# A Linformer attention and MLP-mixer kernel: the first pair's k and v as float32 over two hardware queues, and a new order for the opening

## The chip, the cores and the metric

The kernel runs on one core of a Trainium2 chip. The metric is the device time of one execution in microseconds (us), as the median of several runs. The engines have short names in the profile: PE is TensorE, PEld its weight loads, DVE is VectorE, ACT is ScalarE, POOL is GpSimd and SP is SyncE. A q behind a name (SPq, POOLq) means the engine's instruction sequencer.

## The reference, cut to what matters

```
k_proj = einsum('ks,bhsd->bhkd', E, k)          # q, k, v: 8 x 8 x 1024 x 64
v_proj = einsum('ks,bhsd->bhkd', F, v)          # E, F: 64 x 1024
attn   = softmax(q @ k_proj^T / 8)              # rows of 64 keys
x      = (attn @ v_proj), heads side by side    # 8 x 1024 x 512
h      = relu(x^T @ w_tok1) @ w_tok2            # mixing over the 1024 tokens, 256 wide
u      = x + h^T
out    = u + relu(u @ w_ch1) @ w_ch2            # mixing over the 512 channels, 1536 wide
```

All inputs and the output are float32.

## The kernel before, in words

The batch has eight elements, and each passes through the same stages: the projections of k and v with E and F (`kv_proj`, products in line 521), the transposes of the projected k (`k_transpose`, 574) and of q (`q_transpose_pe`, 618, for the first elements), the scores (637) with their exponential on ACT (652), the product with the projected v (`attend`, 672), whose extra column gives the sum of each row, a reciprocal of that sum (686) and a scaling multiply (692) on DVE that write x. Then come the two products over the tokens, and for each half of 512 tokens (a row block, j from 0 to 15) an up block (1180) and a down block (1289) over the channels, which use seven products of half-size quarters in place of eight. The down block's results are added to u on DVE and stored from the tiles o0, o1 and o2 (1326).

Heads go in pairs, g from 0 to 3 (heads 2g and 2g+1). For batch element 0 the front is done pair by pair, with a token product by parts (`token1_part` 1060, `token2_part` 1092, `u_transpose_pe` 1121), so that the first up block can begin early. The pair g=1, heads 2 and 3, is worked on first.

**What sets the order.** Each piece of work is a job that is handed to a planner (`Planner`, line 116) with its engine and what it reads and writes. The planner schedules nothing any more: the string ORDER lists all jobs in the order in which they are issued, two characters for each job (its number in base 64), SPOTS gives the PSUM bank of each bank user, and FILLS lists the places in that order at which an idle product of zeros (`blank`, line 435) is issued ahead of a PE job. `pin` ties each instruction to the one before it on its engine, so every engine runs its jobs strictly in this order.

**Loads.** k, v, q and the weights come over GpSimd's queue (line 358, `dma`), which casts float32 to bfloat16 on the way; the list LOADS (line 80) names those of batch element 0, two heads for each load, and ORDER says when each is issued. E and F come first of all, as float32, into the tile o0, one over SyncE's queue (257) and one over ScalarE's (258). They are turned on PE with a float32 identity (462) and copied to bfloat16 by ACT and DVE (465). The tiles o1 and o2 (`kv32`, line 259) lie unused in the opening; a switch HWK (90), here 0, would load k and v of heads 0 and 1 into them over the two hardware queues and cast them on DVE and ACT (378 to 390).

**The opening of PE.** Two products of zeros in bfloat16 and two in float32 (`warm`, `warm32`, line 446) keep PE busy while E and F come in; the identities are made on GpSimd meanwhile. Then E and F are turned, then the first pair's q, k and v are worked on as they land.

**Other names that the change touches.** `rdn_t` (295) holds the reciprocals, in two tiles used in turn by pair number. `store` (1315) issues an output store, on GpSimd's queue unless the caller names another; the last row block's stores (`finish`, 1369) name SyncE or ScalarE.

Of the kernel before, what the change touches and what calls it, by code (L numbers as in the profile page):

```python
# [9 lines left out]
F32 = mybir.dt.float32  # L10
# [5 lines left out]
    "0R030T0Q050P0S0408060U070W0V001L0X011M02091E0A1F1G1I1H1J0B1K1N1j1O0C1P1k1c0D1Z1d1Q1e1g1f1h1i0E1R1S1l"  # L16
    "1T1m1W1X0s1U0H0u0w0t0v1n0z0G0x0+1+0F0y0-201-101a1Y24111b1V26250J1812271B19151A1621130I14281C1D1u291o"
    "172S230K2A2T221p1r1q2N2O1v1s2B1t2E1x2P0M2C2U1w2Q1y2V2F1z2R2X2K2W2D2Y2H2G2Z2a2L2I2c2J2b2d2M2l0L2x2m2h"
    "2y2e3B2f2n2i2g2p2o2z3C2q2t2+2-2u2j2r0O302k332v2s0Y37342w310N3L0Z0a353M3d3I3H3D3v323J3N36383R3O0c3E3P"
    "3e0d4c0e3Q3j3K0g3h0f393F3i0b3S3A3f3T3k0h3g3U3-3l3V3G0i3w3X9w3n3W3Y3z4d3m3x3+4u4Y3y4a3p4v4Z403q4g410k"  # L20
    "4w3o5A424x4y0l5B4e0j4h5p4b4f454j464i4k3r5C4z0m43475D5E4l444-0o4m503s4o4n3t4+4p5q525t514B5F4q5r4C495s"
    "530p544D3Z5y3u5w0q5H3bA15x4J3c3a6B5u5I554K5z4r4G4L5K5v4A4H9v5L9x6D484I5+6E0r6F564M6C5-6G6O4N6A606P6Q"
    "626H6I6L4O636561646Z6J674s666K4EA26a57684F6M6b696N4Q0n6f4P6U6g6R6W4R6S6h6Y4U4S6V6c6i6T6X5S4T6d6j6k6u"
    "6l6e5T6m6n6x6+6v5U6o4V6-6y6z716p5a6q4W5G705b725J746r7A73756s765M6t776wA35N7B5O585Q787C5R4t5X5P795Y7J"
    "7F7K7D7G7H7Q7EA57I5Z7L7R5dA759A85eA65VA95fAAA45W5c5h5g5i7V7S5l7TAD7Z7X4X5m5j7a7n5k5n7b7o7W7d5o9z7M7e"
    "7p9-7c7O7q7g7P7r7h7N7f7sAF7i7uAH7Y7lAG7t7m7v7jAJ837wAIANAK7x84ALAOAhAM7z7yAiAP877kAj857U7+88AQAb8986"
    "ARAS8AAcAdAk8BAWAlAm8L9yAZ8CAYAeAT8DAfAaAg8FAUAXAV8M8G8EENB3At7-Az8N8mAEA+8+8i8n8TA-EO8k8oAuAvABAn8H"
    "8U8pB4B5AC8-8q81B0Aq8r92Ao8J90Ap938QArAs8jB6AwB18tB2B795Ax8uB88R8l91Ay8s96B9948v8w9G978x8yBB9H988SBD"
    "999I8KBE9KBCBF8z8WBGEP8VEQ9L9ABABI9N9BBJBH9O9+8X9JBKBNA0BLBO8Y9QBM829MBPBRBSBV8I8aBWBQBTBk9R80BYBXBl"
    "8bBZBUBn9PBc8OBdBa9SBeBfBpBbBh8PBgBmBiER9CBj8ZBo9YEVES9TBr9ZEUBqET8eBs9aEW8f8c9UBu8d9g9W9E9hEYBtC1Bz"  # L30
    "9dEZC2B-9iBwC59VC3BxC69eC48gC89D8hEbC9Bv9bEdC0Ec9c9FEfEj9fCBEeEgEkElCC9jB+EmEhEi9kEn9XEpEr9lC7EoCFCA"
    "By9nCGEsEtCDEq9oCEEu9mCJCHEvEwExCI9r9pCKCXEyEz9qCLCYCME+CNCZEaE-F09sCaILCOCPF19tIMCbDACREXCcF2F4F3Cd"
    "CQ9uF5CeF6CpCfF7FBDCChCSFCDEF9CqDFFADSCiCgFDCrDICTFEDGDJF8FGCjFHFFDHFLDTFICxCkFMFJFPClDUCmFKDLDBDVFQ"
    "FNDDDMFTCVCyINFUFRFODKCnFWDWFXCuDXDNFYCvCzFaCwFVDZFbDQDaC+DRFiFcDODcFSDPFZFdFfFeIPFjFgDdCUFhFlIRDYIT"
    "DkDbISCsIQCWDlFkIUIOC-CoFmFnDeD0CtFoFpDoFqD2DpD1D3FxIXDmD4D6DnIWFzFsFrDrD5FtDqDsFuF-DtD7G0DfDuD8G1Dv"
    "DwF+G2DgG3E0FvG4E1DiDxFwIZE2DyG6IbD+E8G7DjE9IcDzIdGDEAIaE5FyGEG9DhIeGAE6IfD-IhIgGHIiGFIjGIG5GGIkG8IY"
    "GVInE7GKMKIoGBImEBGCGLIsIlECItIuIpGNIqIrIvGOE3IwEDGWE4IxI-GZJ0EEIyGaEFJ1EGIzI+EJEHGXJ5EIJ2GYGcJ3J4GJ"
    "MJGdHQJ7IVJ9J8GbJAD9H8GfGeJBHCGMJCGhJ6JEH9GPJFGiJDGgJJHAHDJGEKHRGQJHJKGRHGJIGTHEHHMLJLMMJNHSJMHUGSHT"
    "HJHVJOGnJPELHFJRHKGjJTEMHXHBJSGlGoJUGpHIJVHMHLJWHNGsGUHYJYHiJQJZHaJXGtHbHOHjJbHPGvJaHmHWJcHnJgJdGwJe"
    "MNGuJfGxGmHZGyMPGkJhHpHcMOJjMRHkMSMQJkGzHlHdHoHqHeJnGqHrJlJoHsGrMVG+HtHuG-JiJzJmH0J+HvH4JpH1JvJsH2H+"  # L40
    "JtJqH3H-HwJxJ-I0JwH5JrK0K1JyJuHyMXK2HxI6MYHgMaK4HzH6I7MZK5HfKBI3I8KCK7MbHhMcK8KDMdQIMeMfKEKFMgMTMhI4"
    "KGK3I5MiK6KIMmI9KJIAMjMkKLIBMnKMK9MoMpKTMlKHKAKUMqI1MrMsQKIDL7MtKXMuMvKZKYIEKKMwL6KVIFKaL8I2IGMxKbMy"
    "KNKWH7ICKdMzKcKeLgM+LAM-IHLBKON0IIN1N3LEN2KfLFKlKgLON5KmLPIJN7KhIKLCN6N8LHMWN4N9LILSL9QHNAKPLQLDNCMU"
    "KiLRNBNDLKLTNENHKRKnLGKjNFLJLVNGKSKqNILLNJLhLMNKLWKrLNNPNLKtNMNQNNKkLiNOKsNSLkNTLYKuKQLZNWLjQJNUNXKw"
    "LlNVKoKvKpNZNRKxNYLUNaNeNbLnNcQLLXNfNdKyKzLaQMNhQOLbNjLmLoNiK+QNLpQPNgQQK-LcLqL0NlLrL2LeL1LsNmLyLtQT"
    "LzLuNnNoL+L3NtLwNxNkM4NyL4NqO9LxL5M5NvOANwNzNuOBM6N+M1NpOCODNrN-OEM2O0NsQVM3O2QWLvO1LdO3M7QXO4O5QYOG"
    "O7OHM8O8QZOFO6M9QaL-OIQdLfOJOLQeQbOKQfMBOMM0QcMCMAQgMDQlQkMFQmMEQnQhORQjP4QUMGP6QiONQRP8OSQoP7P9OXQS"
    "QpQqOVUGPAMHOWQuUFOTPBQvQwOYOUMIQrPCOZQsQtOjPDOaQxQ+PFQyQzObQ-OdR0OcPMOePGOkPNP5PIR1R5PJR3PEOlOPPOPQ"
    "OfPPOrOhR6PHPROsR4R7R2PTR8PSPURAR9RBOoRCPVOpOgUIRFOQRDRGOqPWREPKOtPXPeRJRHOiPfRKRNRLPYRIROOuPLRQPZUH"
    "PiRRPgRcOOPhRSOvRMRTRPRUOwUJRdRVPjRWPaRXUNRfUKRZRYOyULRaRhUMPlRgRbReUOPmPwRiPkRjPnPxRkOzPcPoOmO+PpRl"  # L50
    "RmPyO-PqRnOnRrRoQ2RtOxRvPrQ3RwRpP0Q4RqP1RxP2S7RyPsRzPuUPPbR+P-UQRuPvURS0RsQ0S8S1UUSBUVQ1S9SCS3UWSAQ5"
    "PdUTUXS4SEUYUZUSR-SDSFS2UaSGQ6UbUdS5Q7SJUePtUfUcQ9UgUhSPT3SHSKSQUoQASIUpS6STT2UrUqSUSRT6UsSSQBSWUlUt"
    "QCSXPzUmT7T4P+UnUiQ8TASZUjUkShSLT8UxUuT9QDUvSaUwSVUzQESYU-SiU+V0TBSbT5QFV1TCSNV2QGTDSjUyV4P3TETcScV5"
    "V3TFSpV6SqSdSOV9SfV7VASeTGTdVDSMTKV8THTeSrTIVHTJVBVISmVETLVFVCSnVKTgVLVMThTMSoVJTfVOVGTjTNVPVWTkTOVQ"
    "TiTPVRTlVTSsVNStVUVXTRVSTmTSSgVZVVTQTnVaTuTTToSuSkTpTWTqSwTXSxTYVdVYSySlTsSzTvVeTUSvVbVlTVVgVpVnS+Vf"
    "VqVcS-TwVmVtT0U0VuVoT1W1VhU1W2TaViVwVjVrVxU2W5VkWJW6VvWKTzVyT+WNT-V-W8W0VzU3WOW9W7VsU4WAV+WQTrWPTZWR"
    "WLWSW3WDU5W4X0TtWBWyWTTbWCXIWMWzWVW+WUTxWEX1TyWFU7U6U8WWX4W-U9UBWXWbUAWZX2XaX3UCX5WcXbUDXJX7WYXcWdWH"
    "X6XdWGXMX8WgXNX9WhXPXCXQXAXDXeWiWjXfWaXOXBXEXKXGWmXRXLWIWkXUWlWnXVXhWoWeXiXWXgWqXjWrXmWfXnXkXoXSWsXs"
    "XTWpWtXtXlXHUEXYWuXZXuXpWvXqXFX-XXX+WwXxWxXyXvY9XzXrY0XwY1Y4Y2Y3Y6Y5Y7YAYDY8YBYCYJYFYEYMYGYKYNYHYLYO"
    "YIYPYQ"  # L60
)
SPOTS = (
    "3024101126436327273643040127120236363170420436171063240217145624732113405063774765765024721257605205"
# [5 lines left out]
FILLS = (21, 21, 21, 21, 21, 21, 21, 27, 27, 30, 36, 36, 36, 36, 49, 62, 62, 66, 66, 79, 79)  # L69
# [20 lines left out]
HWK = 0  # L90
# [97 lines left out]
def kernel(  # L188
# [13 lines left out]
    nc = tc.nc  # L202
    P = 128

    B, H, S, D = q.shape
# [37 lines left out]
    def tile_of(shape, dtype, name):  # L243
        return sb.tile(shape, dtype, tag=name, name=name)
# [15 lines left out]
    for i, queue in enumerate((nc.sync, nc.scalar)[:HWK]):  # L260
        queue.dma_start(out=kv32[i], in_=(k, v)[i][0, 0:2].rearrange("h (p si) d -> p h si d", p=P))
# [33 lines left out]
    rdn_t = [tile_of([P, NJ, 2, 2], F32, f"rdn{i}") for i in range(2)]  # L295
# [82 lines left out]
    lead = (1.95, 2.45, 3.2)[HWK]  # L378
    for i in range(HWK):
        pl.add("SPQ", 1.6 + 1.1 * HWK, 1.6 + 1.1 * HWK, lambda: None, writes=[("kv32", i)], prio=-1001)  # L380
        if i:
            act(
                1024, lambda: nc.scalar.copy(out=v_sb[:, 0:2], in_=kv32[1]),
                reads=[("kv32", i)], writes=[("v", 0), ("v", 1)], prio=-100,
            )
        else:
            dve(
                1024, lambda: nc.vector.tensor_copy(out=k_sb[:, 0:2], in_=kv32[0]),
                reads=[("kv32", i)], writes=[("k", 0), ("k", 1)], prio=-100,
            )  # L390
# [55 lines left out]
    opening = [warm(zero), warm(zero), warm32(), warm32()]  # L446
# [7 lines left out]
    opening.append(pl.add("POOL", 1.0, 3.2, identities, writes=["ident"], prio=-150))  # L454
    pl.opening = opening

    for n in range(2):
        b = Bank("S", full=False)

        def turn(n=n, b=b):  # L460
            for i in range(NJ):
                nc.tensor.transpose(bank(b).rearrange("p (i k) -> p i k", i=NJ)[:, i], EF[:, NJ * n + i : S : NSI], ident32)

        def take(n=n, b=b):
            (nc.vector.tensor_copy if n else nc.scalar.copy)(
                out=EFT_sb[:, n * NJ : (n + 1) * NJ].rearrange("p i (e k) -> p i e k", e=2),
                in_=bank(b).rearrange("p (i k e) -> p i e k", i=NJ, e=2),
            )

        pl.add("PE", 0.9, 0.9, turn, reads=["ident"], takes=[b], prio=-150).mms = NJ  # L470
        (dve if n else act)(512, take, writes=[("EFT", n)], uses=[b], prio=-150)
# [185 lines left out]

    def attend(g, half, due, span):
        def unit(jn, due):
            n = len(jn)  # L660
            bk = Bank(stream[0], full=False, span=n)
            rdn = rdn_t[g % 2][:, 2 * half + jn[0] : 2 * half + jn[0] + n]
# [5 lines left out]
            def mm():  # L668
                for k, jj in enumerate(jn):
                    for c in range(2):  # L670
                        at = (2 * half + jj) * P
# [890 lines left out]
```

## Time and profile before

| | before |
|---|---|
| median of 3 runs | 415.22 us (414.95 to 415.27) |
| the profiled execution's own time | 415.69 us |
| its span, from the first to the last instruction | 413.9 us |
| mean granted TensorE clock | 0.999 |
| read from and written to memory | 59.24 MB and 16.78 MB |

The profile is of one execution. A group's row gives the source line, the engine, the operation, output and input by the program's tile names, and the busy time. In rows of a stretch of time the columns are: the stretch, its length, the busy time of each engine with its count of instructions in brackets, the granted clock, the mean share of the 16 DMA engines and the rate at which they wrote, in GB/s. Timeline rows give start, length, engine, line, operation, and in square brackets how long the engine stood idle before and what ended that. Tile names in the profile leave out numbers: `wt_sb` is wt1_sb or wt2_sb, `wc_sb` is one of the channel weights, `o` is one of o0, o1, o2. A DMA's "time to landing" runs from its issue to the moment its data are there.

### The profile page before, as it was taken

Reading aid. Unit: us, or ns where it says so; the run is one execution under the profiler, and the core shown is the slowest. Engines: PE = TensorE matmul, PEld = TensorE weight load, DVE = VectorE, ACT = ScalarE, POOL = GpSimd, SP = SyncE. Lnnn points to the kernel's source line nnn. Section 1 sums busy time; section 2 is a strip of 40 time slices with the busy share of each in tenths; the row PEclk is TensorE's granted clock in tenths of the full one; section 3 lists DMA queues with packets and bytes.
Section 4 is the critical chain, followed back from the end, with each engine's and each line's share of the span. In section 5 each row is a group of like instructions: output and inputs, shape, how many; then the busy total and the mean of one; then the engine's idle time right before and its main releaser. Section 6 shows DMA issues by size and latency. Waiting matters only on the chain.

```text
span 413.9 us, 9589 instructions
## 1 busy us (share of the span) xinstructions
PE 406.4 (98%) x3909; PEld 344.4 (83%) x3911; DVE 355.9 (86%) x773; ACT 221.9 (54%) x429; POOL 66.8 (16%) x105
## 2 busy tenths in 40 slices
PE   8899999999999999999999999999999999999996
PEld 4489888688888888979988899888988798998896
DVE  2289899779999999989979798898989899988686
ACT  1647884258635664574754646455644745445520
POOL 8544021021102120112001112012100001010010
PEclk9999999999999999999999999999999999999999
DMA  8999999997998897978966869873996212251115
GB/s 153 205 202 204 207 190 192 160 172 170 189 166 168 201 170 143 166 156 156 245 118 127 133 148 178 143 167 89 180 227 118 52 51 103 52 115 39 52 69 187
DMA packets 93755, 61.69 MB, mean 149 GB/s; under 512 B 59024, under 2 KB 89232, under 8 KB 93712
## 3 DMA queue, kind: packets, MB, share of 16 engines
q0 software_dynamic: 35088, 45.09, 55.7%
q1 hardware_dynamic: 58256, 15.47, 22.8%
q8 instruction: 30, 0.49, 0.5%
q10 hardware_dynamic: 368, 0.52, 0.3%
q14 instruction: 13, 0.11, 0.1%
HBM read 59.24 MB, written 16.78 MB: 184 GB/s over the span
## 4 chain that ended last, share of the span: by engine, by line
PE 92%; DMA 4%; DVE 2%; POOL 1%; issue 1%; POOLq 0%; DVEq 0%
PE psum L1289 36%; PE psum L1180 35%; PE psum L991 5%; PE psum L875 4%; PE psum L672 3%; PE psum L521 3%; DMA q_sb<-in_q_dram 3%; PE psum L637 2%; DMA v_sb<-in_v_dram 1%; PE psum L712 1%; PE psum L1060 1%; PE psum L736 1%; DVE u L1105 1%; PE psum L1092 1%; PE psum L618 1%
## 5 line engine op out<-in xcount | busy, mean ns | idle before, releaser
L1289 PEld LDWEIGHTS <-G 128*128 128x128 bf16 x1356 | 130.0, 98 | 18.3 <-issue 3.5
L1289 PE MATMUL psum<-wc_sb,G 128*128 128x256 bf16 (+1 forms) x780 | 101.5, 271 | 0.0
L1180 PEld LDWEIGHTS <-wc_sb 128*128 128x128 bf16 x768 | 73.9, 98 | 10.5 <-issue 2.1
L1202 ACT ACTIVATE G<-psum 128x512 bf16<-128x512 f32 x96 | 56.2, 601 | 44.8 <-PE psum L1180 44.3
L1289 PE MATMUL psum<-wT,G 128*128 128x256 bf16 x576 | 75.6, 273 | 0.1
L1216 DVE TENSOR_TENSOR G<-G 128x512 bf16<-128x512 bf16 (+1 forms) x140 | 69.4, 515 | 0.8
L1180 PEld LDWEIGHTS <-wT 128*128 128x128 bf16 x576 | 55.3, 98 | 7.3 <-issue 0.6
L1180 PE MATMUL psum<-S,wc_sb 128*128 128x256 bf16 x384 | 56.2, 273 | 0.0
L1180 PE MATMUL psum<-S,wT 128*128 128x256 bf16 x384 | 56.0, 273 | 0.1
L1180 PE MATMUL psum<-uT,wc_sb 128*128 128x256 bf16 x384 | 55.5, 273 | 0.0
L1326 POOL DMA_DIRECT2D out_dram<-o x30 | 16.4, 548 | 212.7 <-DVE o L1332 171.2
L692 DVE TENSOR_TENSOR x_sb<-psum,rdn 128x256 bf16<-128x256 f32 (+1 forms) x88 | 46.7, 540 | 1.8
L1332 DVE TENSOR_TENSOR o<-psum,u 128x512 f32<-128x512 f32 x59 | 39.9, 681 | 3.7 <-PE psum L1289 3.3
L1208 ACT COPY ub<-psum 128x512 f32<-128x512 f32 x48 | 28.1, 588 | 23.4 <-PE psum L1180 18.5
L652 ACT ACTIVATE a<-psum 128x512 bf16<-128x512 f32 x64 | 34.9, 603 | 8.5 <-PE psum L637 8.3
L1161 DVE CUSTOM_DVE_ANT_0 G<-psum,ub 128x512 bf16<-128x512 f32 x48 | 32.7, 683 | 6.9 <-PE psum L1180 6.6
L1223 ACT COPY psum<-psum 128x512 f32<-128x512 f32 x48 | 27.6, 579 | 18.6 <-PE psum L1180 13.0
L1161 DVE CUSTOM_DVE_ANT_0 G<-psum,ua 128x512 bf16<-128x512 f32 x48 | 32.6, 684 | 5.3 <-PE psum L1180 4.4
L1208 ACT COPY ua<-psum 128x512 f32<-128x512 f32 x48 | 28.3, 590 | 14.0 <-PE psum L1180 13.6
L1180 PE MATMUL psum<-uT,wT 128*128 128x256 bf16 x192 | 28.7, 273 | 0.0
L358 POOL DMA_DIRECT2D v_sb<-in_v_dram x18 | 13.3, 742 | 75.4 <-PE psum L1180 22.7
L672 PE MATMUL psum<-vb,a 128*128 128x130 bf16 x256 | 25.3, 220 | 0.0
(102 smaller groups left out, 499.4 us busy)
## 6 DMA issues: line engine op xcount, KB each, us to landing
out_dram<-o POOLq DMA_DIRECT2D x30, 512.0 KB, 3.8
k_sb<-in_k_dram POOLq DMA_DIRECT2D x14, 512.0 KB, 11.2
v_sb<-in_v_dram POOLq DMA_DIRECT2D x14, 512.0 KB, 7.3
q_sb<-in_q_dram POOLq DMA_DIRECT2D x14, 512.0 KB, 9.2
wc_sb<-in_moe_w_ch_dram POOLq DMA_DIRECT2D x6, 256.0 KB, 11.9
wc_sb<-in_moe_w_ch_dram POOLq DMA_DIRECT2D x4, 384.0 KB, 13.3
k_sb<-in_k_dram POOLq DMA_DIRECT2D x4, 256.0 KB, 7.9
q_sb<-in_q_dram POOLq DMA_DIRECT2D x4, 256.0 KB, 8.1
```

Of the source, the lines that this page charges most:

```text
L652: lambda g=g, half=half, bk=bk: nc.scalar.activation(out=a_t[g][:, half], in_=bank(bk), func=ACT.Exp, scale=scale),
L672: nc.tensor.matmul(view()[:, k, c].rearrange("p i d -> p (i d)"), a_t[g][:, c, at : at + P], vb[:, g].rearrange("k i d -> k (i d)"), start ...
L692: lambda: nc.vector.tensor_tensor(out=x_sb[:, rows, g * P : (g + 1) * P].rearrange("p (n c) (i d) -> p n c i d", c=2, i=2), in0=view()[:, ...
L991: nc.tensor.matmul(view(X_OF[n])[:, r, :], tok2_of(n, i, r), T[n] if n in T else h[B[n]], start=(n in (1, 7) and r == 0), stop=True, skip_ ...
L1161: nc.vector._custom_dve(TENSOR_ADD_SAT, out=out, in0=in0, in1=in1, s0=FMAX, s1=0.0)
L1180: nc.tensor.matmul(t[:, c, :], w1_of(n, dd, 2 * m + c), a_of(j, n, dd), start=(n in (1, 7) and c == 0 and dd == 0), stop=(c == 1 and dd == 1),
L1202: lambda: nc.scalar.activation(out=G[:, n, cs], in_=view(src), func=ACT.Relu),
L1208: 512, lambda: nc.scalar.copy(out=dst, in_=view("y")), writes=[(name, s % 2)],
L1216: 512 * len(both), lambda: f(out=G[:, n, c], in0=G[:, a, c], in1=G[:, b, c]), ps=False,
L1223: 512, lambda: nc.scalar.copy(out=view("y"), in_=view("x")), takes=[bk["y"]],
L1289: nc.tensor.matmul(to, G[:, G_OF[n], cc, t * P : (t + 1) * P], w2_of(n, cc)[:, cut], start=(n in opens and (t == 0 or alone) and cc == 0), ...
L1332: 512, lambda: nc.vector.tensor_add(out=dst, in0=view(src), in1=u_of(sh, dh)),
```

## The change

1. k and v of heads 2 and 3 of batch element 0 (the first pair) are no longer in LOADS. Each of these four heads' slices (256 KB) is loaded as float32 into o1 (k) and o2 (v), head 2 over SyncE's queue and head 3 over ScalarE's, right behind E and F. Each is then cast to bfloat16 on chip: head 2 by DVE, head 3 by ACT.
2. GpSimd's loads in the opening come in another order: k4-5, q2-3, v4-5, q4-5, q0-1, v0-1, k0-1, q6-7, k6-7, v6-7, then the token weights (before: k2-3, q2-3, v2-3, q4-5, k4-5, v4-5, k0-1, v0-1, q0-1, k6-7, q6-7, v6-7). The first six pieces of the up weights change places among themselves.
3. PE opens with one float32 product of zeros fewer. FILLS has 28 entries in place of 21: three ahead of the turning of E and F (place 11), sixteen ahead of the first k/v product (place 24), nine later ones (places 29 to 82). Place 24 is the first pair's k/v product, 29 that of heads 4 and 5.
4. ORDER and SPOTS are new for the opening. Behind it the order on each engine is the one before; all numbers there are four higher.
5. The reciprocals get eight slots in one tile, used in turn, in place of two tiles.
6. The stores of row blocks 13 and 14 go over SyncE's queue in place of GpSimd's.

```diff
-FILLS = (21, 21, 21, 21, 21, 21, 21, 27, 27, 30, 36, 36, 36, 36, 49, 62, 62, 66, 66, 79, 79)
+FILLS = (11, 11, 11, 24, 24, 24, 24, 24, 24, 24, 24, 24, 24, 24, 24, 24, 24, 24, 24, 29, 29, 38, 59, 59, 63,
+    71, 71, 82)
...
-    ("k", 0, 2), ("v", 0, 2), ("q", 0, 2), ("k", 2, 2), ("v", 2, 2), ("q", 2, 2),
+    ("k", 0, 2), ("v", 0, 2), ("q", 0, 2), ("q", 2, 2),
...
-    for i, queue in enumerate((nc.sync, nc.scalar)[:HWK]):
-        queue.dma_start(out=kv32[i], in_=(k, v)[i][0, 0:2].rearrange("h (p si) d -> p h si d", p=P))
+    for i, src in enumerate((k, v)):
+        for h, queue in enumerate((nc.sync, nc.scalar)):
+            queue.dma_start(out=kv32[i][:, h], in_=src[0, 2 + h].rearrange("(p si) d -> p si d", p=P))
...
-    rdn_t = [tile_of([P, NJ, 2, 2], F32, f"rdn{i}") for i in range(2)]
+    rdn_t = tile_of([P, 2 * HP, NJ, 2, 2], F32, "rdn")
...
+    for i, (name, to) in enumerate((("k", k_sb), ("v", v_sb))):
+        pl.add("SPQ", 7.8 + 1.6 * i, 7.8 + 1.6 * i, lambda: None, writes=[("kv32", i)], prio=-1002 + i)
+        for h in range(2):
+            (act if h else dve)(
+                512,
+                lambda i=i, h=h, to=to: (nc.scalar.copy if h else nc.vector.tensor_copy)(
+                    out=to[:, 2 + h], in_=kv32[i][:, h]
+                ),
+                reads=[("kv32", i)], writes=[(name, 2 + h)], prio=-100 + i,
             )
...
-    opening = [warm(zero), warm(zero), warm32(), warm32()]
+    opening = [warm(zero), warm(zero), warm32()]
...
+    attended = iter(range(2 * B * HP))
+
     def attend(g, half, due, span):
+        at = next(attended) // 2 % (2 * HP)
+
         def unit(jn, due):
             n = len(jn)
             bk = Bank(stream[0], full=False, span=n)
-            rdn = rdn_t[g % 2][:, 2 * half + jn[0] : 2 * half + jn[0] + n]
+            rdn = rdn_t[:, at, 2 * half + jn[0] : 2 * half + jn[0] + n]
...
-            queue = queue or nc.gpsimd
+            queue = queue or (nc.sync if NSB - 3 <= j else nc.gpsimd)
```

117 lines of the change are left out of this document (53 added, 64 removed).

## The prediction

> **What bounds the kernel now.** I read the page from the top: busy times, then the chain that ended last.
>
> ```profile
> span 413.9 us, 9589 instructions
> ...
> PE 406.4 (98%) x3909; PEld 344.4 (83%) x3911; DVE 355.9 (86%) x773; ACT 221.9 (54%) x429; POOL 66.8 (16%) x105
> ...
> PE 92%; DMA 4%; DVE 2%; POOL 1%; issue 1%; POOLq 0%; DVEq 0%
> ```
>
> TensorE (PE) is busy 98% of the span and holds 92% of the chain; only 4% is DMA. A busy PE may still be waiting inside a row, so the next view is who PE waited for, and the stretches between. First the waits of PE and of its weight loads (PEld) from 24.13 to 46 us, all the rows there are: line, what for, us in total, times, longest.
>
> ```profile
> PE psum L1060 <- DVE x_sb L692: 0.2, 1, 0.2
> ```
>
> ```profile
> PEld L1060 <- issue: 0.5, 2, 0.3
> PEld L1180 <- DVE wT L476: 0.3, 1, 0.3
> ```
>
> One microsecond of waits in 22 us: from the first token product (L1060) at 24.13 PE runs almost without a gap. Ahead of that it is different. These are the stretches of the fill products alone (L436, products of zeros whose result nobody uses): us, PE busy and count.
>
> ```profile
> 9.90:24.13 14.23, 4.27 (x15) 1.08 (x14) 1.00 1.21 206
> 24.13:46.00 21.87, 0.00 (x0) 0.00 (x0) 1.00 1.31 203
> ```
>
> Fifteen fills take some 4.3 of the 14.2 us before 24.13, and none comes later. Since the order behind the opening is fixed and PE is full in it, **the time is the moment at which PE becomes full plus the work left then**. So I look for what sets 24.13: the chain of waits in its order of time (start, us, what) and the first token product.
>
> ```profile
> 3.87 6.17 DMA v_sb<-in_v_dram
> ...
> 10.34 11.12 DMA q_sb<-in_q_dram
> ...
> 31.84 1.29 DVE u L1105 x2
> ```
>
> ```profile
> 23.75 0.10 PEld L1060 LDWEIGHTS <-wt_sb 128*128 128x128 bf16 x1
> 24.13 0.61 PE L1060 MATMUL psum<-x_sb,wt_sb 128*128 128x128 bf16 x8 [0.16 <-DVE x_sb L692]
> ```
>
> ```profile
> L358 POOL DMA_DIRECT2D wt_sb<-in_moe_w_tok_dram x1: 561/561/561, 12.9 to 12.9; - x1
> ...
> DMA to landing us min/median/max: 10.7/10.7/10.7
> ```
>
> The chain is two loads of GpSimd's queue, landing at 3.87 + 6.17 = 10.04 and 10.34 + 11.12 = 21.46. The first half of wt1 is issued at 12.9 and lands 10.7 later, 23.6; the token product that reads it loads weights at 23.75. **The opening is paced by one stream of loads.** From 31.84 the chain lies on VectorE (DVE), up to the wait of 0.3 for wT among PEld's waits above, so DVE is the second bound. The stream itself, by stretches (last number GB/s written, the one before it the engines' share):
>
> ```profile
> 2.00:3.00 1.00, 1.00 (x2) 0.15 (x1) 0.00 (x0) 0.63 (x1) 0.86 (x5) 1.00 0.78 213
> 3.00:4.00 1.00, 1.00 (x4) 0.63 (x3) 0.00 (x0) 0.00 (x0) 1.00 (x3) 1.00 0.86 311
> 4.00:5.00 1.00, 1.00 (x3) 0.42 (x2) 0.00 (x0) 0.00 (x0) 1.00 (x2) 1.00 0.99 141
> 5.00:7.00 2.00, 2.00 (x9) 1.39 (x7) 0.00 (x0) 0.34 (x1) 2.00 (x4) 1.00 1.20 192
> 7.00:9.50 2.50, 1.79 (x16) 1.05 (x15) 1.38 (x2) 0.24 (x1) 2.50 (x4) 1.00 0.95 148
> 9.50:23.60 14.10, 12.19 (x142) 6.49 (x140) 4.96 (x21) 8.65 (x20) 7.05 (x11) 1.00 1.22 206
> ```
>
> Steady, the stream writes 206 GB/s: a load of two heads (256 KB written as bfloat16, 512 KB read) each 262/206 = 1.27 us. In 4 to 9.5 it is not full: 65 + 2 x 14 + 2.5 x 58 = 238 KB short, which is 238/206 = **1.16 us of room**.
>
> **The change, part by part.** *The two loads.* k and v of heads 2 and 3 leave GpSimd's queue (2 x 1.27 = 2.54 us of stream) and come as four float32 loads of 256 KB on SyncE's and ScalarE's queues, behind E and F. They read as much from memory as before but write 1.05 MB instead of 0.52. No row shows such a load; the nearest are E and F.
>
> ```profile
> L258 ACTq DMA_DIRECT2D o<-in_F_dram x1: 563/563/563, 0.8 to 0.8; - x1
> ...
> DMA to landing us min/median/max: 3.2/3.5/3.8
> ```
>
> F is issued at 0.8 and lands at 0.8 + 3.8 = 4.6. In 3 to 4 us, with E and F in flight, 311 GB/s are written: more than 206, so float32 bytes go faster than cast ones. If an engine's time follows the bytes read, the four take 1.05/0.412 = 2.54 us, what the two removed give back, and the stream gains whatever room they fill: at most 1.16. If it follows the bytes written, they take 1.05/0.206 = 5.1 us, and the stream's end moves 2.54 later less the room. Between -1.16 and +2.54 I take **-0.8**: nearest to the 311 row, but the new loads share the engines only until about 9 us, so part of the 7 to 9.5 hole stays. All later loads keep their number in the stream (k of heads 6 and 7 becomes eleventh, after q; wt1 stays thirteenth), so wt1, wt2 and wc1 move by the same 0.8: wt1's first half to 22.8. GpSimd's issuing is no bound: 0.56 us in wt1's row, under the stream's 1.27; its order decides only which load comes first.
>
> A rule that speaks against this: the Trainium skill, page "DMA: Bandwidth & Descriptors", section "Issuing engines are not separate DMA queues", says that DMAs from the scalar, sync and gpsimd engines run on the same 16 DMA engines and interleave, so that issuing from several saves only the sequencer's time. By it alone the stream would gain nothing; the room in 4 to 9.5 is the trace's evidence that the one queue did not keep the engines full.
>
> *The first pair's start.* PE's opening loses a float32 fill and gets 3 + 16 fills.
>
> ```profile
> 1.13 4.64 PE L436 MATMUL psum<-zero 128*128 128x512 f32 x6 [1.13 <-DVE zero L303]
> ...
> 3.00 0.15 PEld L436 LDWEIGHTS <-zero 128*128 128x128 bf16 x1 [0.70 <-issue]
> ...
> 3.43 0.76 PEld L436 LDWEIGHTS psum<-zero 128*128 128x128 f32 x2 [0.28 <-issue]
> ...
> 5.56 1.58 PE L462 MATMUL psum<-ub,o 128*128 128x128 f32 x8
> ...
> 8.31 1.67 PE L436 MATMUL psum<-zero 128*128 128x512 bf16 x7
> ...
> 9.91 0.24 PE L521 MATMUL psum<-k_sb,EFT_sb 128*64 128x128 bf16 x1
> ```
>
> The two bfloat16 fills are 0.43 apart, so of the 5.56 - 1.13 = 4.43 us each float32 fill has (4.43 - 0.86)/2 = 1.79. Without one, PE is done at 3.77; three fills at 0.43 bring 5.05, past F's landing at 4.6; the turning of E and F ends 1.58 later, 6.6; sixteen fills at 1.67/7 = 0.24 end at 10.4. So the first k/v product starts near **10.4 instead of 9.91**, whenever its data are there between 6 and 10. That costs nothing at the end: the first pair is done long before 22.8, and what is late in the opening is the last pair. If v came after 10, pair 1 would be as much later, and PE, which takes its work in order, with it; the later waits for loads, the last pair's at 21.46 - 0.8 the last of them, take up some microseconds of that.
>
> *The casts.* Four of 128x512, two on DVE, two on ScalarE (ACT), against rows of that size:
>
> ```profile
> 6.66 0.59 ACT L465 CAST EFT_sb<-psum 128x512 bf16<-128x512 f32 x1 [4.03 <-PE psum L462]
> ...
> 7.18 0.69 DVE L465 CAST EFT_sb<-psum 128x512 bf16<-128x512 f32 x1 [5.30 <-PE psum L462]
> ```
>
> ```profile
> 0.00:9.90 9.90, 8.06 (x29) 4.15 (x29) 2.25 (x7) 1.87 (x2) 8.36 (x18) 1.00 0.79 151
> 9.90:24.13 14.23, 12.16 (x143) 6.73 (x143) 5.46 (x23) 9.11 (x21) 7.32 (x11) 1.00 1.21 206
> 24.13:31.75 7.62, 7.51 (x127) 7.38 (x127) 7.02 (x23) 3.01 (x8) 3.44 (x5) 1.00 1.38 198
> 31.75:39.00 7.25, 7.19 (x88) 6.47 (x87) 7.02 (x17) 5.28 (x11) 3.78 (x5) 1.00 1.30 204
> ```
>
> At most 4 x 0.69, on engines busy 2.25 and 1.87 of the first 9.9 us: hidden. They do add waits: ACT's first cast stands ahead of its copy of the turned E and F, DVE's ahead of the other, and the first product needs both anyway. ACT issues three loads at about 0.56 before its table load (at 1.35), which moves some 1.1 later, while its first work was at 6.66. SyncE has nothing else queued.
>
> *The order.* An order string holds two characters per job, its number in base 64. Seven jobs are added ahead, two loads and one fill go, so every later number grows by four; read so, PE's order equals the old one from its 107th job on, DVE's from its 89th, ACT's from its 61st. The next batch element's first k/v product goes seven jobs further back, behind products of the up block, so its loads get time as PE comes earlier. Within the opening the second pair's product follows the first directly, and all four attention products of heads 4 and 5 (L672) stand ahead of the first token product, where two stood behind it. A unit of four:
>
> ```profile
> 23.56 0.23 PEld L672 LDWEIGHTS <-a 128*128 128x128 bf16 x4 [0.23 <-issue]
> ```
>
> so 2 x 0.23 = **0.46 of PE work is done in the waiting time**. DVE gets as far: five instead of one of the scaling multiplies (L692) stand ahead of the last pair's kb copies. But DVE is busy 7.02 of 7.62 and 7.02 of 7.25 us behind 24.13; with 0.83 us of slack it can follow the stream's 0.8 and little more. I keep 0.3 of the 0.46.
>
> *The rest.* Eight slots of rdn instead of two: the same instructions, in order on one engine that nobody waits for by that tile; 0. The stores of row blocks 13 and 14 go from GpSimd to SyncE:
>
> ```profile
> 369.55 3.30 SPq L784 DMA_TRANSPOSE uT<-u  x1
> ```
>
> ```profile
> 404.40 0.53 POOL L1326 DMA_DIRECT2D out_dram<-o  x1 [2.68 <-DVE o L1342]
> ...
> 408.05 3.27 SPq L1326 DMA_DIRECT2D out_dram<-o  x4
> ```
>
> SyncE's last transpose is issued at 369.55 + 3.30 = 372.85, ahead of the moved stores, of which the last goes out at 404.4; the final ones follow at 408.05 and set the end: 0. If the moved store delayed SyncE's first final issue, 0.5 us at most.
>
> **Sum**: -0.8 (stream) - 0.3 (order) = -1.1 us. The profiled execution took 415.69 (span 413.9); 415.69 - 1.1 = 414.59, which lies 0.47 over the median as 415.69 does, so 415.22 - 1.1 = **414.1**.
>
> **The rivals.** *Nothing gained in the stream*: the four loads take the engines from the cast loads as fast as they relieve them. Speaks for it: the share column is already about 1 in 4 to 9.5. Against: 148 GB/s beside 206. Then only the order's 0.3, at most 0.46, is left: 414.9. The skill's rule named above would end here.
>
> *More than I count*: the room is all filled (1.16), the 0.46 stays, and of the 4.3 us of fills some more goes, because the order places nine fills behind the first product instead of fourteen (5 x 0.24 = 1.2, of which half may be real): 1.16 + 0.46 + 0.6 = 2.2, 413.0. Against: DVE's slack of 0.83.
>
> *Slower*: the engines pay by bytes written. Then +2.54, less room 1.16 and less 0.3 in order = +1.1, **416.3**; without any room 417.5. It decides where the float32 loads write below 1.05/(2.54 + 1.16) = 284 GB/s. For it: in 2 to 3, at E's start, 213 are written. Against: that stretch holds the start of the first load, and 311 follows it.
>
> *The change doesn't do what it says*: the first pair isn't earlier at all (10.4), so that the name of the change gives nothing. That is already in my sum, and is no case of its own.
>
> **How the numbers follow.** Forecast 0.5 (stream 0.5 to 1.1 earlier: 413.6 to 414.6); nothing gained 0.2; more 0.14; slower 0.16. A measurement of this kernel can tell about 0.2%, 0.83 us, so faster means under 414.39, slower over 416.05. Of the forecast's 0.5 some 0.42 lies below 414.39: faster 0.42 + 0.14 = 0.56. Slower: of its 0.16 some 0.13. Same: 0.31. The range leaves out the far end of "more" and nearly all of "slower": 412.9 to 415.8; the forecast's own is 413.6 to 414.6.
>
> **What would show it.** Right: the first half of wt1 lands near 22.8 and the first L1060 product starts near 23.3 (was 24.13); 4 to 9.5 us above 190 GB/s; the first L521 product near 10.4; no new row in the waits of PE behind 24. Wrong: the float32 loads landing after 10, wt1 at 23.6 or later, DVE waits of L1180 growing beyond 0.3, or the final SyncE issues waiting for the moved store.

## The result, and the profile after

| | before | after |
|---|---|---|
| median | 415.21 us (414.31 to 416.59, 22 runs) | 416.0 us (415.54 to 416.36, 22 runs) |
| profiled execution, its own time | 415.69 us | 415.89 us |
| its span | 413.9 us | 414.1 us |

The ratio after/before is **1.0017, 95% interval 1.0011 to 1.0024**: some 0.7 to 0.8 us slower, a small loss, but clear of the noise, where 414.1 (412.9 to 415.8) had been forecast. Of those 0.8 us the two profiled executions show 0.2: before's lies 0.48 over its median, after's 0.11 under.

The page of after, its span, its busy times and the chain that ended last by engine:

```profile
span 414.1 us, 9614 instructions
...
PE 407.0 (98%) x3914; PEld 345.1 (83%) x3916; DVE 357.2 (86%) x775; ACT 223.6 (54%) x431; POOL 63.2 (15%) x99
...
PE 94%; DMA 3%; POOL 1%; DVE 1%; issue 0%; ACT 0%; POOLq 0%; DVEq 0%
```

DMA's share of the chain fell from 4 to 3% and PE's rose from 92 to 94: loads pace the opening less, and the span is no shorter. The stretches of the stream in after (last number GB/s, ahead of it the engines' share):

```profile
2.00:3.00 1.00, 1.00 (x2) 0.15 (x1) 0.00 (x0) 0.55 (x1) 0.85 (x5) 1.00 0.86 160
3.00:4.00 1.00, 1.00 (x4) 0.35 (x3) 0.00 (x0) 0.73 (x1) 1.00 (x3) 1.00 0.98 381
4.00:5.00 1.00, 1.00 (x4) 0.48 (x3) 0.00 (x0) 0.00 (x0) 1.00 (x2) 1.00 1.11 312
5.00:7.00 2.00, 2.00 (x14) 1.52 (x13) 0.00 (x0) 1.21 (x2) 2.00 (x4) 1.00 1.05 256
7.00:9.50 2.50, 2.50 (x13) 1.07 (x11) 1.03 (x2) 0.42 (x1) 1.17 (x2) 1.00 1.14 274
9.50:22.70 13.20, 11.32 (x143) 6.87 (x142) 6.53 (x23) 8.76 (x21) 6.96 (x10) 1.00 1.22 206
```

From 4 to 9.5 us the rates went from 141, 192 and 148 to 312, 256 and 274. The room is filled, and the first half of wt1 comes earlier: its load, alone in a view of 12 to 13 us,

```profile
L359 POOL DMA_DIRECT2D wt_sb<-in_moe_w_tok_dram x1: 558/558/558, 12.3 to 12.3; - x1
...
DMA to landing us min/median/max: 10.4/10.4/10.4
```

is issued at 12.32 and lands at 22.7, where 22.8 was forecast and 23.6 was before. Yet the first token product hardly moved. PE's timeline in after, with rows left out at the dots:

```profile
19.22 0.62 PE L618 MATMUL psum<-ident,q_sb 128*128 128x128 bf16 x8 [0.50 <-DMA q_sb<-in_q_dram]
...
20.35 0.38 PE L436 MATMUL psum<-zero 128*128 128x512 bf16 x1
20.66 0.63 PE L521 MATMUL psum<-k_sb,EFT_sb 128*64 128x128 bf16 x8
21.23 0.43 PE L676 MATMUL psum<-vb,a 128*128 128x130 bf16 x4
21.59 0.63 PE L521 MATMUL psum<-v_sb,EFT_sb 128*64 128x128 bf16 x8
...
22.35 0.88 PE L676 MATMUL psum<-vb,a 128*128 128x130 bf16 x8
23.34 0.41 PE L637 MATMUL psum<-qT,kT 64*64 64x512 bf16 x4
...
24.02 1.17 PE L1064 MATMUL psum<-x_sb,wt_sb 128*128 128x128 bf16 x18 [0.27 <-DVE x_sb L696]
```

and the same place in before, where the first token product starts at 24.13:

```profile
21.50 0.62 PE L618 MATMUL psum<-ident,q_sb 128*128 128x128 bf16 x8 [0.45 <-DMA q_sb<-in_q_dram]
21.96 0.62 PE L672 MATMUL psum<-vb,a 128*128 128x130 bf16 x8
22.51 0.63 PE L521 MATMUL psum<-v_sb,EFT_sb 128*64 128x128 bf16 x8
23.22 0.41 PE L637 MATMUL psum<-qT,kT 64*64 64x512 bf16 x4
23.57 0.40 PE L672 MATMUL psum<-vb,a 128*128 128x130 bf16 x4
```

In both, the transposes of the last q (L618) are the last products for which PE waits for a load. That wait ends 2.28 us earlier in after, 19.22 instead of 21.50. But 4.80 us of work on PE, DVE and ACT lie between it and the first token product, where there were 2.63. Part of this is an exchange: q of heads 6 and 7 now comes ahead of k of these heads. By issue and time to landing, their k, q and v land at 19.0, 21.5 and 22.3 in before, and at 20.2, 19.2 and 21.5 in after.

A fairer mark is the last product that reads one of these loads, that of v of heads 6 and 7 (the second L521 row in after, the only one in before). It starts at 21.59 instead of 22.51, so the forecast 0.8 is there. From it to the first token product there are 2.43 us instead of 1.62, and this difference takes the gain back. What fills that stretch is read from the busy times in it (PE, PEld, DVE, ACT, POOL), first in after, then in before:

```profile
21.59:24.02 2.43, 1.88 (x24) 1.41 (x23) 2.31 (x11) 1.13 (x3) 1.48 (x2) 1.00 1.12 210
```

```profile
22.51:24.13 1.62, 1.37 (x18) 0.96 (x17) 1.55 (x7) 1.12 (x2) 1.08 (x2) 1.00 1.10 206
```

DVE is busy 2.31 of 2.43 us there, with eleven operations where there were seven: the new order has copies of the last pair's k and v and more of the scaling multiplies there, ahead of the first token product. The chain of waits of after leads back past all this:

```profile
7.41 11.76 DMA q_sb<-in_q_dram
...
24.02 1.28 PE psum L1064 x20
```

The last load on the chain, that q, lands at 7.41 + 11.76 = 19.17; wt1 is on it in neither kernel. Behind 24, the waits of PE that are left:

```profile
PE psum L1064 <- DVE x_sb L696: 0.3, 1, 0.3
```

So PE is full from 24.02 on, as forecast, and then the two kernels do the same work. The up block is reached a little earlier, because less is left to do behind the first token product:

```profile
33.47 0.71 PE L1184 MATMUL psum<-uT,wc_sb 128*128 128x256 bf16 x5
```

against 33.95 for the same product in before. Of that 0.48 us (0.37 from 52 us on, product against product) nothing is left at the end: laid over before's, after's products stand 0.32 us earlier up to 296 us, 0.04 earlier at 302 and 0.20 later from 322 to the last one. Two places take it. The first is at 300 us, ACT's timeline in after and in before:

```profile
297.94 0.59 ACT L1212 COPY ub<-psum 128x512 f32<-128x512 f32 x1
299.94 0.37 ACT L910 COPY u<-psum 128x256 f32<-128x256 f32 x1 [1.41 <-PE psum L1184]
```

```profile
298.27 0.59 ACT L1208 COPY ub<-psum 128x512 f32<-128x512 f32 x1
299.99 0.37 ACT L906 COPY u<-psum 128x256 f32<-128x256 f32 x1 [1.13 <-PE psum L875]
```

PE's product (L879, L875 in before) needs this copy of u. At 298 us ACT is 0.33 us ahead of before; at the copy only 0.05. The second place is at 320. PE's timeline in after, then in before:

```profile
319.61 0.82 PE L1293 MATMUL psum<-wc_sb,G 128*128 128x256 bf16 x6
320.51 0.92 PE L1293 MATMUL psum<-wT,G 128*128 128x256 bf16 x7
```

```profile
319.65 0.82 PE L1289 MATMUL psum<-wc_sb,G 128*128 128x256 bf16 x6
320.31 1.15 PE L1289 MATMUL psum<-wT,G 128*128 128x256 bf16 x9
```

0.90 us from one start to the next instead of 0.66. VectorE had waited there for a transpose of u, which landed 5.8 us after its issue, where it took 4.4 in before:

```profile
DVE S L811 <- DMA uT<-u: 0.6, 1, 0.6
```

### The profile page after: what moved, and what is told of

It is laid out like the page before. It is cut to its first block, busy times and chain, and to the rows that moved or that the text cites. A ratio compares the mean times of both kernels' runs of the same rounds, so it can differ in the third digit from the quotient of the medians.

```text
span 414.1 us, 9614 instructions
## 1 busy us (share of the span) xinstructions
PE 407.0 (98%) x3914; PEld 345.1 (83%) x3916; DVE 357.2 (86%) x775; ACT 223.6 (54%) x431; POOL 63.2 (15%) x99
## 3 DMA queue, kind: packets, MB, share of 16 engines
q10 hardware_dynamic: 656, 1.05, 0.8%
## 4 chain that ended last, share of the span: by engine, by line
PE 94%; DMA 3%; POOL 1%; DVE 1%; issue 0%; ACT 0%; POOLq 0%; DVEq 0%
PE psum L1293 36%; PE psum L1184 36%; PE psum L995 5%; PE psum L879 5%; PE psum L676 3%; PE psum L521 3%; DMA q_sb<-in_q_dram 3%; PE psum L637 2%; PE psum L1096 1%; PE psum L1064 1%; PE psum L716 1%; PE psum L740 1%; PE psum L618 1%; POOL q_sb L359 1%; PE psum L1125 0%
## 5 line engine op out<-in xcount | busy, mean ns | idle before, releaser
L1184 PEld LDWEIGHTS <-wc_sb 128*128 128x128 bf16 x768 | 73.9, 98 | 10.4 <-issue 2.1
L1330 POOL DMA_DIRECT2D out_dram<-o x26 | 14.3, 549 | 177.1 <-DVE o L1336 124.3
```

Source lines behind the costliest of these rows:

```text
L1184: nc.tensor.matmul(t[:, c, :], w1_of(n, dd, 2 * m + c), a_of(j, n, dd), start=(n in (1, 7) and c == 0 and dd == 0), stop=(c == 1 and dd == 1),
```

## The experiments

Each trace has the same products on PE behind the opening, so two traces are laid one over the other, product by product. Three moments are compared below: the landing of wt1's first half, the start of the first token product, and the start of the up block. Times are medians; a ratio is against before, run on the same chip.

### Which part costs it: stores, slots, opening

e1 is before with the moved stores alone, e3 before with the eight slots alone; e2 is after with the stores back on GpSimd, e4 after with the stores back and the two old tiles of reciprocals. The edit shown is e2's.

```diff
-            queue = queue or (nc.sync if NSB - 3 <= j else nc.gpsimd)
+            queue = queue or nc.gpsimd
```

> The kernel before, with only the stores of row blocks 13 and 14 moved from GpSimd's to SyncE's queue. Theory A (the small parts outside the opening cost the time: stores and reciprocals together +0.8 to +1.2 us, which hides an opening that gains 0.4): 0.3 to 1.0 us slower than before. Theory B (the new opening itself is dearer, through what it shifts in the steady part behind it): within 0.2 us of before, 415.2.

> The changed kernel with the stores of row blocks 13 and 14 back on GpSimd's queue. Theory A, if the stores are the cost: 0.3 to 1.0 us below the changed kernel's 416.0. Theory B: 416.0 within 0.2.

> The kernel before, with only the reciprocals in one tile of eight slots instead of two tiles. Theory A, if the reciprocals are the cost (fewer waits on a slot but other memory addresses): 0.3 to 1.0 us slower than before. Theory B: within 0.2 us of before, 415.2.

> The changed kernel with the reciprocals in two tiles and the stores on GpSimd's queue as before: only the opening and its order are new. Theory A: 414.8, the 0.4 us by which the changed kernel's products stand earlier from 52 us on in the two traces, since what was lost later is gone. Theory B: 416.0 within 0.2, and in the trace the products stand 0.3 to 0.5 us earlier at 52 us and lose that again by steps in the steady part.

| kernel | median, us | ratio, 95% interval |
|---|---|---|
| before | 415.52 | |
| e1, stores alone | 415.94 | 1.0007 [0.9997, 1.0017] |
| e3, slots alone | 415.37 | 0.9997 [0.9984, 1.0009] |
| e2, after without the stores' move | 416.46 | 1.0023 [1.0013, 1.0032] |
| e4, after without stores and slots | 416.88 | 1.0032 [1.0019, 1.0045] |

Taking the small parts out does not bring the time back (e2, e4): the cost comes with the new opening and what it shifts behind it. The expectations were only partly met: e1's 0.4 lies between its two theories, with an interval that includes no change, e2 lies above what either gave, and so does e4, forecast at 414.8 or 416.0. Two traces say how. In e2 the last row block's stores land later; its issues in the last 8 us, then those of after in the same stretch (median us to landing at the end of the row):

```profile
out_dram<-o SPq DMA_DIRECT2D x2, 128.0 KB, 2.7
```

```profile
out_dram<-o SPq DMA_DIRECT2D x2, 128.0 KB, 2.2
```

The last product of e2 stands within 0.03 us of after's, but its span ends 0.76 later. So in this trace the stores' move is worth more than half a microsecond at the end, which it was not in before; by the ratios, 1.0023 and 1.0017 with overlapping intervals, it is less. In e4 DVE waits at 146 us, for a transpose of u:

```profile
DVE S L811 <- DMA uT<-u: 1.3, 1, 1.3
```

That wait put PE 1.36 us back. In before, e3, after and e2 the same transpose landed at 143.1, 143.4, 144.8 and 144.8; it is needed at about 145.2. Here the margin was gone. It is not a matter of the new opening alone: in e1 and in f1 (below), both with the old opening, it landed at 145.3 and 145.5, and PE lost 0.2 us. Why it lands so late in some kernels was not settled.

### Loads without the order, order without the loads

g4 is before's loads in the new order, with 7 unused ACT copies to keep ACT's count of instructions. g3 is the reverse: the order of before with the float32 loads and casts; it keeps after's slots and moved stores, and has 7 unused ACT copies and two 32-byte loads on GpSimd besides. g5 is g3 with fourteen fills ahead of the first q product in place of seven ahead of the first k/v product.

```diff
 (g5 against g3)
-FILLS = (26, 26, 26, 26, 26, 26, 26, 32, 32, 35, ...)
+FILLS = (18, 18, 18, 18, 18, 18, 18, 18, 18, 18, 18, 18, 18, 18, 32, 32, 35, ...)
```

> The new order, its fills and eight slots of reciprocals, with heads 2 and 3 of k and v as cast loads on GpSimd ahead of the others (as before the change), no casts on chip, no store moved; seven one-column copies on ScalarE keep its pause harmless. If the new order lives on the loads' earlier landing (it waits last for q at 19.2 us and has 4.8 us of work behind that): the first token product 0.6 to 0.9 us later than the changed kernel's 23.85, the up block near 34.0 (33.3), time 415.9. If the order alone brings the gain and the loads nothing: up block near 33.4, time 415.2.

> The order before, with heads 2 and 3 of k and v as float32 over the two hardware queues and cast on chip as in the changed kernel (their casts around the copies of the turned E and F; q of heads 2 and 3 first on GpSimd); seven one-column copies on ScalarE and two loads of 32 bytes on GpSimd keep the pauses where the unchanged kernel had them harmless. Theory of the prediction (the stream's 0.8 us reach the end): the first half of wt1 lands near 22.5, the first token product starts near 23.0 (four executions of the old opening: 23.4 to 24.2, mean 23.8) and the first up block near 32.9 (mean 33.7), time 414.6. Rival (TensorE's own work and its fills fill the time behind the last loads, so that an earlier wt1 has nothing to give): wt1 lands near 22.5 as well, but the first token product near 23.5 and the up block near 33.3, time 415.1 or more.

> The kernel of the loads alone (the order of before, k and v of heads 2 and 3 as float32 over the hardware queues, seven one-column ACT copies and two 32-byte loads that nobody uses), with its 7 fills ahead of the first k/v product replaced by 14 ahead of the first q product, so that PE does not stand idle for 3.4 us there and the clock has no cause to fall (it was 0.79 between 9.5 and 23.6 us). If the idle PE and the low clock were all that made the loads alone slow: clock 1.0 throughout, wt1's first half landing near 22.3, and no trace of the 3.5 us. Then the two theories on what the loads are worth: the prediction's stream theory has the first token product 0.9 earlier than the mean of the old opening, 22.9, the up block at 32.8 and the time 0.9 under before, 414.3; the theory of PE's own work (in its fixed order PE reaches the last pair's products only after the first pair's, which start about 1 us later here) has the first token product at 23.5 to 24.5, the up block at 33.3 to 34.3, and the time between 0.4 under and 0.6 over before. If the old order of work is itself what cannot stand loads that land later at the start, the first token product is behind 25 and the time over 416.5 at full clock.

| kernel | wt1's first half lands | first token product | up block | median, us | ratio |
|---|---|---|---|---|---|
| old opening, 4 executions | 23.4 (22.8 to 23.9) | 23.83 (23.36 to 24.22) | 33.67 (33.2 to 34.07) | | |
| g4, order alone | 23.1 | 24.35 | 33.79 | 415.95 | 1.0007 [0.9999, 1.0015] |
| g5, loads alone, filled | 22.66 | 24.88 | 34.74 | 416.63 | 1.0021 [1.001, 1.0032] |
| g3, loads alone | 22.1 | 27.65 | 37.51 | 418.21 (415.88 to 419.16) | 1.005 [1.0035, 1.0065] |
| new opening, 7 executions | 22.6 (22.4 to 22.7) | 23.86 (23.69 to 24.02) | 33.32 (33.14 to 33.47) | | |

The old opening's four are before, e1, e3, f1; the new one's seven are after, e2, e4 and four below. g4 came out near the first of its two expectations (an order that lives on the loads' earlier landing), g5 near the last of its three. g5 is the clearest of all. wt1 lands 0.7 us earlier than in the old opening, and the first token product is 1.05 us later. Its load of wt1, and the start of its chain of waits, which names no DMA at all from 0 to 26 us:

```profile
L362 POOL DMA_DIRECT2D wt_sb<-in_moe_w_tok_dram x1: 558/558/558, 12.8 to 12.8; - x1
...
DMA to landing us min/median/max: 9.9/9.9/9.9
```

```profile
1.13 4.63 PE psum L439 x6
5.77 1.42 PE psum L465 x8
7.19 3.02 PE psum L439 x14
10.21 0.46 PE psum L621 x8
...
22.10 0.60 ACT a L655
...
24.40 0.76 DVE x_sb L699 x2
```

The path runs from the first fill through PE, ACT and DVE to the token product. (The fourteen fills end at 10.21 and the first q had landed at 9.8, so up to 0.4 of the 1.05 is the fills' own doing.) The up block shifts by 34.74 - 33.67 = 1.07, and the run loses 416.63 - 415.54 = 1.09, but that the two agree is partly luck: laid over before's trace, product by product, g5 stands 0.68 us later at 52 us and 0.73 at 310, so the opening's shift is carried, and another 0.35 is lost at 320, where the transpose of u is late here too.

The old and the new order differ by the same amount in every trace. From the start of the last v product to the first token product it is 1.59 to 1.63 us in the five traces with the old order (g5 among them) and 2.36 to 2.43 in the eight with the new one (g4 among them); on to the up block it is 11.41 to 11.49 against 11.82 to 11.91. g3, at its lower clock, is left out of both. So behind the last load the new order takes **0.43 us more**. Ahead of it, the last v product starts at 22.23 in the mean of the four old openings and at 21.44 in that of the seven new ones, 0.78 earlier; and 0.78 - 0.43 is the 0.35 at the up block. In g4 that product starts at 21.92, in g5 at 23.25.

g3's expectation missed in size. There PE waited 3.44 us for ACT's copy of the turned E and F, which stood behind ACT's cast of k, and its granted clock was 0.79 in the mean behind that; the first row is PE's timeline, the second the stretch with the granted clock ahead of the last two columns:

```profile
9.93 1.01 PE L621 MATMUL psum<-ident,q_sb 128*128 128x128 bf16 x8 [3.44 <-ACT EFT_sb L468]
```

```profile
9.50:23.60 14.10, 12.71 (x118) 6.58 (x117) 3.33 (x12) 7.10 (x18) 7.68 (x11) 0.79 1.22 208
```

In after the order puts sixteen fills in that place, which end at 9.7, about when the casts are done. So neither half is worth anything alone: the loads cost 0.7 to 1.1 us in the old order, the new order alone about nothing (0.1 later at the up block, one execution against a scatter of 0.9), and together they are worth 0.35, of which the loads bring 0.47 on top of the order (33.32 beside the 33.79 of g4's one execution).

### What takes the 0.35 back: ACT at 300 us

The change adds two loads, two casts and their waits to ACT's program. If the extra time at 300 us hangs on the number of an instruction in that program, then adding instructions to before must bring it, and adding some to after must take it away. f1 is before with 8 unused one-column ACT copies in the opening, f3 after with 3, f4 after with 8 unused GpSimd memsets in the middle, f2 with both of these.

```diff
+    spare = tile_of([P, 1], F32, "spare")
+    for _ in range(3):
+        nc.scalar.copy(out=spare, in_=zero[:, :1])
```

> The kernel before, with eight copies of one column added on ScalarE in its idle time ahead of 6 us (their result is not used). Theory P (engines pause at fixed numbers of their own instruction stream; the change moved the pauses to instructions that others wait for): the copy of u for the token product at 300 us becomes the same instruction of ScalarE's stream, by number, as in the changed kernel, so the 0.29 us wait of TensorE there, which the old opening never showed, appears: 0.2 to 0.4 us slower than before. Rival theory D (the loss at 300 us comes from the earlier arrival of the work itself, against a transfer chain that does not come earlier): no wait of TensorE at 300 us beyond the 0.19 of before, time of before within 0.2.

> The changed kernel with three copies of one column added on ScalarE ahead of its first cast and eight one-column memsets on GpSimd ahead of its first output store (results not used), which move both engines' instruction numbers. Theory P: ScalarE's pause falls on a copy that nobody waits for and GpSimd's 0.96 us pause no longer on the store at 287 us that holds back five loads; the waits at 300 and 320 us go, 0.5 us less than the changed kernel: 415.5. Theory D: both waits stay, 416.0.

> The changed kernel with the three copies on ScalarE alone. Theory P: the wait at 300 us goes, that at 320 us stays; 0.29 us less than the changed kernel, 415.7. Theory D: no change, 416.0.

> The changed kernel with the eight memsets on GpSimd alone. Theory P: the store at 287 us starts 0.30 us after the VectorE instruction that it waits for instead of 1.26, the transposes of q behind it come 1 us earlier, the wait at 320 us goes, that at 300 us stays; 0.24 us less, 415.8. Theory D: no change, 416.0.

| kernel | ACT copies, memsets added | late copy at 300 us | median, us | ratio |
|---|---|---|---|---|
| before | | no | 415.41 | |
| f1, before with 8 ACT copies | 8, 0 | yes | 415.84 | 1.0013 [0.9996, 1.0031] |
| f2, after with both | 3, 8 | no | 415.57 | 1.0002 [0.999, 1.0014] |
| f3, after with 3 ACT copies | 3, 0 | no | 415.34 | 0.9999 [0.9987, 1.0011] |
| f4, after with memsets | 0, 8 | yes | 416.0 | 1.0008 [0.9992, 1.0024] |

The rows of that copy in f1 and in f3, in ACT's timeline:

```profile
300.00 0.37 ACT L909 COPY u<-psum 128x256 f32<-128x256 f32 x1 [1.41 <-PE psum L1183]
```

```profile
299.36 0.37 ACT L913 COPY u<-psum 128x256 f32<-128x256 f32 x1 [1.13 <-PE psum L882]
```

Idle ahead of the copy: 1.41 us in after and, with 8 instructions added, in the order of before; 1.13 in before and, with 3 added, in the order of after. This holds both ways and is shown: the longer pause is there in all five traces in which the copy is the 448th instruction that the trace records of ACT's program (after, e2, e4, f4 and f1), and in none of the others (440th in before, e1 and e3, 451st in f2, f3 and the g runs). PE's wait for it in f1, which f3 does not have:

```profile
PE psum L878 <- ACT u L909: 0.2, 1, 0.2
```

In the times, f4's median lies 0.66 and 0.43 us over those of f3 and f2 in the same batch, more than the 0.28 that the traces place here; f1's interval includes no change.

What makes the pause is not shown. One candidate is the fetch of instructions. The page of after has 14 such fetches of 8 KB on one queue and does not say for which engine. By their times, five come just behind ACT's recorded instructions 69, 191, 319, 450 and 575, some 128 apart; the others do not fit such a spacing. But the fourth of these starts at 303.1, after the late copy. The Trainium skill, page "Runtime: NRT & Kernel Launch", section "Instruction fetch mechanics", says that a sequencer refills its instruction memory in blocks of 256 instructions and that the cost of crossing one is mostly hidden. Here the fetches that follow ACT's count are some 128 instructions apart; no run shows what one of them costs.

### GpSimd's pause, and the wait at 320 us

One store in after starts 1.26 us behind its DVE operation, where all others need 0.30. In before the same 0.96 us lies on a load at 271; both are GpSimd's 79th DMA. g1 is f3 with two 32-byte loads added on GpSimd ahead of both places, so that by the count of DMAs the pause must go back to the load at 270.

```diff
+                    nc.gpsimd.dma_start(out=t, in_=E[:1, :8]) for t in (spare_d if j == 0 and sh == 0 else ())
```

> The changed kernel with three copies of one column added on ScalarE ahead of its first cast and two loads of 32 bytes added on GpSimd ahead of its first output store (results not used). Theory Q (GpSimd's pause of 0.96 us comes at its 79th DMA, whatever stands between; the change took two DMAs away ahead of it and so moved it from a load of v at 271 us to the store at 287 us): the pause goes back to the load of v, the store starts 0.30 us after its VectorE instruction, and with ScalarE's pause moved as well neither the wait at 300 nor that at 320 us is there: 415.1, which is the changed kernel less 0.5 and more. Rival: the pause belongs to that store or to its time; then the wait at 320 us stays and the time is that of the kernel with the three copies alone, 415.3.

g1 ran in **415.38** us (414.94 to 415.65) beside 415.62, ratio **0.9986 [0.9974, 0.9998]**, the lowest ratio of the study. GpSimd's timeline in after and in g1, around the store:

```profile
287.49 0.55 POOL L1330 DMA_DIRECT2D out_dram<-o  x1 [13.67 <-DVE x_sb L696]
288.06 0.75 POOL L359 DMA_DIRECT2D v_sb<-in_v_dram  x1
```

```profile
286.42 0.55 POOL L1336 DMA_DIRECT2D out_dram<-o  x1 [12.70 <-DVE o L1342]
287.97 0.75 POOL L363 DMA_DIRECT2D v_sb<-in_v_dram  x1 [1.00 <-issue]
```

The pause did not go back. It moved the other way, by one instruction, onto the load behind the store, GpSimd's 82nd DMA; the 79th, at 269.67, is not late. So the theory of the count of DMAs failed: the pause is at the 79th in eleven traces and at the 82nd in the three with the two small loads (g1, g3, g5). The count of instructions does not set it either, since f2's and f4's memsets did not move it. What does is open. And its place was worth nothing: the wait at 320 stayed with the store on time,

```profile
DVE S L815 <- DMA uT<-u: 0.7, 1, 0.7
```

so the theory that this pause causes it fell too. The transpose behind it, issued near 313, has two durations to landing and nothing between: 4.3 to 4.4 us in before, e1, f1 and g3, where DVE doesn't wait, and 5.8 to 6.1 in e3, g5 and all eight traces with the new order, where it waits 0.6 to 0.9. What holds it up stays open; neither the loads (g4 has the old ones) nor the order (e3 and g5 have the old one) is needed for it. That g1 is faster than f3 is not shown either: f3's interval reaches from 0.9987 to 1.0011, its median is 415.34, and in the two traces g1's products stand 0.2 to 0.3 us later.

## Why the prediction was wrong, point by point

- **PE is full from the first token product, and the work behind is fixed** (step 1). The first half held: PE has no wait over 0.3 us behind 24 up to 46 us, and after's lead over before stays between 0.37 and 0.32 from 52 to 296 us. The second half failed by 0.5 to 0.7 us (0.28 at 300 and 0.2 to 0.4 at 320): the work behind is the same, the time for it is not. A pause on ACT that moves with the count of its instructions fell on a copy that PE needs, and a transpose took the longer of two durations.
- **The stream, -0.8**. The size was right: wt1's first half landed at 22.7 (22.6 in the mean of seven, where four old openings have 23.4), the rates between 4 and 9.5 are above 190 GB/s, and the last v product starts 0.78 earlier in the mean. (How this divides between the loads and q's new place is not settled: g4, with the order alone, has 0.3 of it, in one execution.) Wrong was to carry this to the first token product by way of wt1. That product came at 23.86 in the mean of seven, 23.83 before. The landing of wt1 was not what set it; it stood beside a chain that ended at nearly the same time, from the last q through PE and DVE. The prediction's own chain showed it: its last load is q, landing at 21.46, and then comes PE's and DVE's work.
- **The order, -0.3, done in waiting time**. This is the step that failed in the opening, and its sign is wrong: behind the last v product the new order takes 0.43 longer to the up block, in all eight traces that have it. The L672 units that it moves ahead of the first token product bring their DVE work with them, and copies of the last pair's k and v stand there too. DVE is busy 2.31 of the 2.43 us between the last v product and the first token product, so this is no waiting time. Which of its operations costs how much was not tried one by one. The prediction had named DVE as the second bound, with 0.83 us of slack, and kept the 0.3 all the same. That the two terms together give 0.35 at the up block, near the forecast 0.3 of this one, is luck. And the order alone (g4) gained nothing; it needs the loads, which in the old order (g5) cost 0.7 to 1.1 us.
- **The first product at 10.4, costing nothing**. It came at 9.67 for k and 10.16 for v, near the forecast. In g5, where the first pair's k/v product starts at 11.51 instead of 9.91, PE's work is behind all the way to the up block and no load is on its chain. So "what is late in the opening is the last pair" does not hold in every order: PE takes its work in order, and the first pair's products stand at its head.
- **Casts hidden**: held in after but for 0.25 us, the wait of the first v product for DVE's cast, since sixteen fills cover them; in g3, without that cover, ACT's cast held PE for 3.44 us. That ACT's casts and loads move its whole later program by eight instructions, and with it the pause, was in no step. It costs 0.28 at 300.
- **Slots 0**: held (e3). **Stores 0, at most 0.5**: in before they bring nothing or cost 0.4 (e1, interval with zero); in the new opening they save up to 0.5 (416.46 without, 416.0 with, in two batches). Both are within the bound of 0.5, if on either side of 0.
- **The rival "nothing gained in the stream"** gave 414.9 by another mechanism. The rule it cited from the Trainium skill, page "DMA: Bandwidth & Descriptors", section "Issuing engines are not separate DMA queues", would have the stream no faster; the rates of 312 and 274 where 141 and 148 stood, and the 0.8 by which wt1 lands earlier, speak for room that one queue had left. (The rates count bytes written, of which a float32 load has twice as many.) The gain was lost behind the stream, not in it.

So on the traces: about 0.35 won in the opening instead of 1.1 (0.78 by the last v product, less 0.43 behind it), 0.28 lost at 300, 0.2 to 0.4 at 320, which sums to between 0.1 and 0.3 slower. The medians say 0.8 slower. The rest, about half a microsecond, is not placed; old openings alone differ by 0.86 us from one execution to the next, and one trace of each kernel can't settle it.

## What to carry to other kernels

A load that lands just when its user starts is not thereby what the user waits for. Follow the chain back from the user, find the last load on it, and count the work that lies between, on every engine; an order that puts more of it there spends what a faster stream has won. When an order is moved together with a stream, do each alone before the two are credited, and lay the traces over one another, product by product, to the end: what an opening wins can be lost 250 us later, as at the ACT copy that is late only by its number in the program.

## What had not been expected of the hardware

- A pause of 0.28 us on ACT moved with the number of instructions in front of it, by 8 one-column copies in one direction and by 3 in the other.
- GpSimd paused some 0.96 to 1.00 us in every trace, at its 79th DMA in eleven and at its 82nd in the three with two small loads added; memsets did not move it. What sets its place is open.
- The same transpose of u landed 4.3 to 4.4 us after its issue or 5.8 to 6.1, with nothing between, in all fourteen traces; the cause is open.
- After 3.44 us without a matmul the granted clock was 0.79 in the mean from 9.5 to 23.6 us (g3); a row of eight transposes took 1.01 us, where the first such row in g5, at a clock of 1.00, took 0.61.
- Float32 loads on two hardware queues, together with the cast queue, wrote 381 GB/s between 3 and 4 us and 274 from 7 to 9.5, where the cast queue alone wrote 206 in its steady part.
